# Attention of a fused kernel in plain float32 on quarters of TensorE's array, with scores and values in one stretch

## The chip, the cores and the metric

One core of a Trainium2 chip runs one program. The metric is the device time of one execution in microseconds (us), the median of the runs shown. Engines are named as the profile names them: PE is TensorE (PEld its weight load), DVE VectorE, ACT ScalarE, POOL GpSimd, and SP SyncE, which only issues DMAs here.

## The reference

Banded attention with a bias by distance, then an MLP whose activation is a ratio of two polynomials, on 8 x 576 = 4608 tokens:

```python
scores = q @ k.T / sqrt(64)              # 8 batches, 8 heads, 576 positions, head size 64
mask = (0 <= rel) & (rel < 128)          # rel = query position - key position
p = softmax(where(mask, scores - slope[h] * abs(rel), -1e9))
x = (p @ v)                              # heads side by side: 4608 tokens x 512
h = x @ w_in                             # 512 x 2048, float64 given
P = a0 + a1*h + a2*h*h + a3*h*h*h
Q = 1 + abs(b0)*abs(h) + abs(b1)*h*h
out = (P / (Q + 1e-6)) @ w_out           # 2048 x 512
```

## The kernel before

The 4608 tokens are 36 blocks of 128. The MLP goes over tiles of blocks, `MLP = [3] + [2]*15 + [3]`. Tile 0 is computed with float32 matmuls. From tile 1 on, an operand is a sum of a high and a low part in a rounded type (fp32r), and a product is three matmuls: hi x hi, lo x hi, hi x lo (up, L603; down, L659). The float64 weights arrive as pairs of 32-bit words and are put together on the chip by `convert(k)`, k = 0 to 31 (POOL L560, ACT L561, DVE L562 and L563), whose PSUM tile `cv` lies in the banks `sc0` and `sc1` for k >= 4. This work fills the time of tile 0. `split(k)` then makes the high and low parts.

Attention runs one tile ahead of the MLP: that of tile t+1 is issued among the matmuls of tile t. Its unit is a pair of heads p (heads 2p and 2p+1, whose 64 channels each fill the 128 partitions) and one or two query blocks. A query of block i sees only keys of blocks i-1 and i, so one 128 x 128 matrix holds all of its weights: keys of its own block on and under the diagonal, and keys of the block ahead over it. For each unit:

- `job(u)` loads keys and queries into `kq_raw` (L384) and the values into `v` (L385). From tile 1 on ACT makes `kq_hi` (L386) and DVE `kq_lo` (L387).
- Scores (L430): for each block and head a matmul over 64 rows, one row half of PE's array for each head, against 256 keys, three times (hi x hi, lo x hi, hi x lo), into the banks `sc0` and `sc1`.
- DVE merges the two blocks of keys with a predicated copy (L444) and takes bias and maximum (L450); ACT exponentiates (L455); DVE makes the reciprocal of the sum (L463, L464); POOL multiplies (L465).
- PE transposes the four matrices into `pt` (L476), ACT copies them to `p_all` (L480), and POOL parts them again into own and previous block with two affine selects (L484).
- Values (L509): float32 matmuls over 128 keys, one column half of the array (64 columns) for each head, into `px`. `px` and `pt` take turns in one bank, `ptx`. ACT copies `px` to `x_hi` (L520), DVE makes `x_lo` (L522).

A float32 matmul stands as two records in the trace, an fp32r matmul as one. Scores and values of a unit stand at different places of PE's order, each among matmuls of the MLP on the whole array.

The order of each engine comes from `Plan`, a list scheduler in Python that runs when the program is built: each operation has a due time and an estimated cost, and at each step an engine takes the ready operation that is due first and whose buffers are free. Due times come from constants (`A0` to `BL`, L265 to L271). Each engine then runs its instructions in that order and waits at each for its inputs.

## Time and profile before

| what | us |
|---|---|
| median of 3 runs (lowest, highest) | 1065.49 (1064.55, 1065.85) |
| the profiled execution's span, first to last instruction | 1062.6 |
| PE busy in it | 1037.1 (98%) |
| DVE busy | 834.6 (79%) |
| ACT busy | 707.4 (67%) |
| POOL busy | 520.4 (49%) |
| start, to the first up-projection of tile 0 | 41.2 |
| from there to the last down-projection of tile 0 | 110.2 |
| from there to the last matmul | 907.0 |
| after it | 4.2 |

The span is 2.9 us under the median of the runs. Busy times are sums over the span; the stretches in the lower half of the table differ in what limits them, so each is read by itself. PE's overlapping matmuls count once in its busy time, but a group's mean duration counts the whole way of one matmul through the array, so the pace of a row of matmuls is read from the distance of their starts.

### The profile page before, as it was taken

What the parts mean: (1) busy time and instruction counts of PE and PEld (TensorE: products, weight loads), DVE (VectorE), ACT (ScalarE), POOL (GpSimd) and SP (SyncE); (2) the same over time, 40 slices, a digit from 0 to 9 for tenths busy, and PEclk for the clock granted to TensorE, in tenths of its full rate; (3) what the DMA queues carried; (4) which work ended last, traced back from release to release, by engine and by line L of the source; (5) the groups of instructions that cost most, each with busy time, mean ns of one, the idle gap of its engine ahead of it and who ended that gap; (6) DMA issues with size and microseconds to landing.
All of it is one profiled execution on the core that took longest, in us unless ns stands there. A gap on an engine that the chain in (4) does not pass through costs nothing.

```text
span 1062.6 us, 19670 instructions
## 1 busy us (share of the span) xinstructions
PE 1037.1 (98%) x6863; PEld 861.3 (81%) x6863; DVE 834.6 (79%) x1989; ACT 707.4 (67%) x1642; POOL 520.4 (49%) x578
## 2 busy tenths in 40 slices
PE   7799899999999999999999999999999999999998
PEld 4554467888888888888888888888888888888997
DVE  4798799978787877878787868687878787786776
ACT  5676788666766666757575757666666766685664
POOL 3744579744544453545353444444444545454442
PEclk8899999999999999999999999999999999999999
DMA  9625421011111120202020111112121211020000
GB/s 304 226 70 179 139 92 53 24 58 38 64 40 63 41 75 27 80 24 75 21 72 29 60 52 48 63 33 68 38 73 34 68 43 58 28 74 6 21 1 30
DMA packets 45267, 68.78 MB, mean 65 GB/s; under 512 B 4464, under 2 KB 29936, under 8 KB 45168
## 3 DMA queue, kind: packets, MB, share of 16 engines
q1 hardware_dynamic: 45168, 67.52, 19.8%
q8 instruction: 54, 0.88, 0.3%
q14 instruction: 45, 0.37, 0.1%
HBM read 58.07 MB, written 9.44 MB: 64 GB/s over the span
## 4 chain that ended last, share of the span: by engine, by line
PE 85%; DVE 4%; DMA 4%; POOL 3%; ACT 2%; issue 1%; SPq 0%; DVEq 0%; POOLq 0%; ACTq 0%
PE h L603 36%; PE acc L659 35%; PE px L509 6%; PE sc L430 5%; PE pt L476 2%; DMA raw_w<-in_w_in 2%; POOL w_lo L578 1%; DMA raw_w<-in_w_out 1%; DVE w L563 1%; DMA kq_raw<-in_kqv 1%; POOL p_all L484 1%; POOL g_q L629 0%; ACT pr L455 0%; DVE cv L562 0%; DVE g_p L630 0%
## 5 line engine op out<-in xcount | busy, mean ns | idle before, releaser
L603 PE MATMUL h<-x_hi,wi_hi 128*128 128x256 f32 (+1 forms) x1024 | 308.2, 301 | 0.0
L603 PE MATMUL h<-x_lo,wi_hi 128*128 128x256 f32 (+1 forms) x1024 | 290.7, 284 | 0.0
L627 POOL TENSOR_SCALAR g_q<-g_u,babs 128x512 f32<-128x512 f32 (+1 forms) x152 | 116.0, 763 | 330.1 <-ACT g_u L626 321.0
L603 PE MATMUL h<-x_hi,w_lo 128*128 128x256 f32 (+1 forms) x960 | 272.6, 284 | 0.7 <-POOL w_lo L578 0.7
L603 PEld LDWEIGHTS h<-x_hi,wi_hi 128*128 128x128 f32 x1024 | 192.4, 188 | 39.1 <-issue 8.8
L603 PEld LDWEIGHTS h<-x_lo,wi_hi 128*128 128x128 f32 x1024 | 192.6, 188 | 37.4 <-issue 1.0
L659 PE MATMUL acc<-wo_hi,g_h 128*128 128x512 f32 x528 | 209.0, 396 | 1.3 <-ACT g_h L643 1.3
L659 PE MATMUL acc<-w_lo,g_h 128*128 128x512 f32 x495 | 194.9, 394 | 0.0
L659 PE MATMUL acc<-wo_hi,g_l 128*128 128x512 f32 x528 | 193.3, 397 | 0.0
L629 POOL TENSOR_TENSOR g_q<-g_q,g_u 128x512 f32<-128x512 f32 (+1 forms) x152 | 188.5, 1240 | 9.6
L603 PEld LDWEIGHTS h<-x_hi,w_lo 128*128 128x128 f32 x960 | 181.2, 189 | 1.2 <-POOL w_lo L578 0.9
L626 ACT ACTIVATE g_u<-h 128x512 f32<-128x512 f32 (+1 forms) x152 | 87.4, 575 | 136.0 <-PE h L603 134.6
L635 DVE SCALAR_TENSOR_TENSOR g_q<-g_q,h 128x512 f32<-128x512 f32 (+1 forms) x152 | 99.4, 654 | 81.4 <-ACT h L634 80.1
L632 ACT ACTIVATE g_u<-g_q,guard 128x512 f32<-128x512 f32 (+1 forms) x152 | 107.0, 704 | 69.1 <-POOL g_q L629 68.2
L630 DVE TENSOR_TENSOR g_p<-h,g_p 128x512 f32<-128x512 f32 (+1 forms) x152 | 100.5, 661 | 53.0 <-ACT g_p L628 52.6
L644 DVE TENSOR_TENSOR g_l<-h,g_h 128x512 fp32r<-128x512 f32 (+1 forms) x136 | 90.9, 668 | 51.4 <-ACT g_h L643 49.9
L484 POOL TENSOR_SCALAR_AFFINE_SELECT p_all<-p_all 128x512 f32<-128x512 f32 (+1 forms) x144 | 95.9, 667 | 71.2 <-ACT p_all L480 66.7
L455 ACT ACTIVATE pr<-pr,st 128x128 f32<-128x128 f32 x288 | 112.8, 396 | 13.5 <-DVE st L450 13.4
L465 POOL TENSOR_TENSOR pr<-pr,st 128x512 f32<-128x512 f32 (+1 forms) x76 | 76.6, 1008 | 84.8 <-DVE st L464 55.3
L628 ACT ACTIVATE g_p<-h,na 128x512 f32<-128x512 f32 (+1 forms) x152 | 114.9, 756 | 0.0
L636 DVE SCALAR_TENSOR_TENSOR h<-g_p,na,h 128x512 f32<-128x512 f32 (+1 forms) x152 | 109.3, 719 | 0.0
L631 DVE SCALAR_TENSOR_TENSOR g_p<-g_p,na,h 128x512 f32<-128x512 f32 (+1 forms) x152 | 108.1, 711 | 1.0
(76 smaller groups left out, 1799.9 us busy)
## 6 DMA issues: line engine op xcount, KB each, us to landing
kq_raw<-in_kqv SPq DMA_DIRECT2D x64, 320.0 KB, 2.9
v<-in_kqv SPq DMA_DIRECT2D x68, 192.0 KB, 2.5
out<-o SPq DMA_DIRECT2D x33, 256.0 KB, 2.2
raw_w<-in_w_in SPq DMA_DIRECT2D x16, 512.0 KB, 5.4
raw_w<-in_w_out SPq DMA_DIRECT2D x16, 512.0 KB, 4.0
bias_t<-in_bias SPq DMA_DIRECT2D x44, 64.0 KB, 2.3
kq<-in_kqv SPq DMA_DIRECT2D x4, 320.0 KB, 4.9
kq_raw<-in_kqv SPq DMA_DIRECT2D x4, 192.0 KB, 2.4
```

The costliest lines, as they stand in the source:

```text
L455: nc.scalar.activation(ap(pr)[:, y, :], ap(pr)[:, y, :], AF.Exp, bias=ap(st)[:, y : y + 1], scale=-1.0, accum_out=ap(st)[:, 4 + y : 5 + y])
L484: plan.op(A + D2 + 0.6 - 0.1 * k, cost, lambda e, k=k, sign=sign: nc.gpsimd.affine_select(out=side(k), in_=side(0), pattern=[[0, 2], [0, m ...
L603: nc.tensor.matmul(h(n), w[:, k, :], x[:, k, :], start=(k == 0 and m == 0), stop=(k == NKC - 1 and m == len(seq) - 1))
L627: plan.op(E, {"g": tsc}, lambda e: nc.gpsimd.tensor_scalar(v(g_q), v(g_u), ap(babs)[:, 1:2], ap(babs)[:, 0:1], ALU.mult, ALU.add), reads=[ ...
L628: plan.op(E, {"a": act(W, 1, 2) - 20}, lambda e: nc.scalar.activation(v(g_p), v(h_s), AF.Identity, bias=ap(na)[:, 2:3], scale=ap(na)[:, 3: ...
L629: plan.op(E, {"g": ttc}, lambda e: nc.gpsimd.tensor_tensor(v(g_q), v(g_q), v(g_u), ALU.mult), reads=[(g_q, 0), (g_u, 0)], writes=[(g_q, 0)])
L630: plan.op(E, {"v": dve(W)}, lambda e: nc.vector.tensor_tensor(v(g_p), v(h_s), v(g_p), ALU.mult), reads=[(h_s, 0), (g_p, 0)], writes=[(g_p, ...
L631: plan.op(E, {"v": dve(W, 1)}, lambda e: stt(v(g_p), v(g_p), ap(na)[:, 1:2], v(h_s), ALU.add, ALU.mult), reads=[(h_s, 0), (g_p, 0)], write ...
L632: plan.op(E, {"a": act(W, 0, 1)}, lambda e: nc.scalar.activation(v(g_u), v(g_q), AF.Ln, bias=guard, scale=1.0), reads=[(g_q, 0)], writes=[ ...
L635: plan.op(E, {"v": dve(W)}, lambda e: stt(v(g_q), v(g_q), GUARD, v(h_s), ALU.add, ALU.mult), reads=[(g_q, 0), (h_s, 0)], writes=[(g_q, 0)])
L636: plan.op(E, {"v": dve(W, 1)}, lambda e: stt(v(h_s), v(g_p), ap(na)[:, 0:1], v(h_s), ALU.add, ALU.mult), reads=[(g_p, 0), (h_s, 0)], write ...
L659: nc.tensor.matmul(ap(accs[t][i]), x[:, sl], w, start=(c == 0 and part == 0 and m == 0), stop=(c == NFC - 1 and (part == 1 or t == 0) and ...
```

## The change

All of attention is in plain float32, and `kq_hi` and `kq_lo` are gone. The array is used in quarters of 64 rows x 64 columns. A unit is now always two blocks (two of one pair, or one block of two pairs), which makes 6, 15 x 4 and 6 units, where there were 8, 15 x 4 and 8. For a unit's scores each quarter (row half = head h, column half = half g of the queries) multiplies 192 keys per block: in one piece for g = 0, in pieces of 128 and 64 for g = 1, so that keys which a query half can't see are left out. For its values each quarter (row half = half b of the keys, column half = head) takes four matmuls of 128, 128, 64 and 64 columns. From tile 1 on, the values of unit u-2 and the scores of unit u are one operation of the plan, in the same PSUM tile `sc` of two banks, of which there is one; columns 384 to 511 of each bank hold the values. `pt` is alone in `ptx`.

```diff
+    def values(u, bank):
+        (v, w, w2), keys = stage[u]
+        def run():
+            for n, (own, k, part) in enumerate(((1, 0, 0), (0, 1, 0), (0, 0, 1), (1, 1, 1))):
+                for b in range(2):
+                    r = slice(64 * b, 64 * b + 64)
+                    for h in range(2):
+                        c = slice(64 * h, 64 * h + 64)
+                        q = slice(3 * P + 64 * k, 3 * P + 64 * k + 64) if part else slice(3 * P, 4 * P)
+                        y = ap(w2)[r, k, h] if part else ap(w)[r, 2 * P * k + P * h : 2 * P * k + P * h + P]
+                        nc.tensor.matmul(bank(b)[c, q], ap(v)[r, own, k, c], y, start=(n == 0), stop=(n == 3), tile_position=(64 * b, 64 * h))
+        return run
...
+        back = u - LAG if u - LAG >= first_unit[1] else None
+        if back is not None:
+            small.append(values(back, bank))
...
+            def scores():
+                for b in range(2):
+                    for g, k0, w, at in ((0, 0, 192, 0), (1, 128, 128, 0), (1, 64, 64, 128)):
+                        for h in range(2):
+                            r, c = slice(64 * h, 64 * h + 64), slice(64 * g, 64 * g + 64)
+                            nc.tensor.matmul(bank(h)[c, 192 * b + at : 192 * b + at + w], qt(b)[r, c], kt(b)[r, k0 : k0 + w], start=True, stop=True, tile_position=(64 * h, 64 * g))
...
+        plan.op(A, {"p": cost}, lambda e: [f() for f in small], reads=reads, writes=sk, rows=0.9)
```

The values of a unit of tile 0 stay an operation of their own. The two affine selects become a multiplication by a mask into `p_far` and a subtraction, of 256 elements a partition each. The masks come by one more DMA at the start, cast by DVE; the predicated copies wait for them too. `v` is loaded by four DMAs of 64 partitions instead of one of 128:

```diff
-                plan.op(A + D2 + 0.6 - 0.1 * k, cost, lambda e, k=k, sign=sign: nc.gpsimd.affine_select(out=side(k), in_=side(0), pattern=[[0, 2], [0, m], [sign, P]], compare_op=ALU.is_ge, fill=0.0, base=k - 1, channel_multiplier=-sign), reads=[(w, 0)], writes=[(w, k)])
+        plan.op(A + D2 + 0.5, cost, lambda e: nc.gpsimd.tensor_tensor(ap(w2), mixed(), far(), ALU.mult), reads=[(w, 0), (masks, 0)], writes=[(w2, 0)])
+        plan.op(A + D2 + 0.6, cost, lambda e: nc.gpsimd.tensor_tensor(mixed(), mixed(), ap(w2), ALU.subtract), reads=[(w2, 0), (w, 0)], writes=[(w, 0)])
...
+        plan.op(-7, {"s": 182}, lambda e: eng[e].dma_start(ap(masks16), bias[4, :, :2]), writes=[(masks16, 0)])
+        plan.op(-7, {"v": 300}, lambda e: nc.vector.tensor_copy(ap(masks), ap(masks16)), reads=[(masks16, 0)], writes=[(masks, 0)])
...
+            for g in range(2):
+                eng[e].dma_start(ap(v)[64 * b : 64 * b + 64, :, g], part[64 * g : 64 * g + 64].rearrange("r (j c) -> r j c", j=2))
```

`cv` of the conversions moves into the two banks of `sc`, k even and odd of a chunk in one tile, and the plan's constants are new:

```diff
-        cv = slot(ps1, [P, DM], I32, "cv", tag=f"acc{k % 2}" if k < 4 else f"sc{k % 2}")
+        elif k % 2 == 0:
+            cv_s = cvs[c] = slot(ps1, [P, 2, DM], I32, "cv", tag="sc")
...
-    AOFF, D2, D3, JL, VL = -0.563, 3.406, 5.885, 9.935, 4.671
+    AOFF, D2, D3, JL, VL = -0.5917, 3.483, 6.45, 11.305, 4.987
```

PE in the steady part, before: the values of one unit (L509) and, further on, the scores of another (L430), among up-projections (L603) and down-projections (L659).

```order
L603 MATMUL h<-x_hi,w_lo_1418 128x256
L509 MATMUL px<-p_all,v 64x256 x2
L509 MATMUL px<-p_all,v 64x128 x4
L603 MATMUL h<-x_hi,wi_hi 128x256
...
L603 MATMUL h<-x_hi,w_lo_1457 128x256
L430 MATMUL sc_4864<-kq_hi 128x256
L430 MATMUL sc_4866<-kq_hi 128x256
L430 MATMUL sc_4864<-kq_lo,kq_hi 128x256
L430 MATMUL sc_4866<-kq_lo,kq_hi 128x256
L430 MATMUL sc_4864<-kq_hi,kq_lo 128x256
L430 MATMUL sc_4866<-kq_hi,kq_lo 128x256
```

PE in the steady part, after: one stretch of values (L409) and scores (L463), among up-projections (now L625) and down-projections (L681).

```order
L681 MATMUL acc_4629<-wo_hi,g_l 128x512
L409 MATMUL sc<-p_all,v 64x128 x8
L409 MATMUL sc<-p_far,v 64x64 x8
L463 MATMUL sc<-kq 64x192 x2
L463 MATMUL sc<-kq 64x128 x2
L463 MATMUL sc<-kq 64x64 x2
L463 MATMUL sc<-kq 64x192 x2
L463 MATMUL sc<-kq 64x128 x2
L463 MATMUL sc<-kq 64x64 x2
L625 MATMUL h<-x_hi,wi_hi 128x256
```

The two stretches of a unit have become one, the six matmuls of 128 keys have become sixteen of 64, and the twelve fp32r matmuls of 256 keys twelve float32 matmuls of 64 to 192.

SP at the start of the program, before: keys and queries of four pairs, then values one DMA at a time, `id_sb` (the identity) and the first weights (`raw_w`).

```order
L364 DMA kq_first<-in_kqv 128x256 x3
L310 DMA bias_first<-in_bias 128x1024
L364 DMA kq_first<-in_kqv 128x256
L365 DMA v_first<-in_kqv 128x128
L373 DMA kq_96<-in_kqv 128x640
L365 DMA v_first<-in_kqv 128x128
L308 DMA id_sb<-in_ident 128x256
L365 DMA v_first<-in_kqv 128x128
L373 DMA kq_122<-in_kqv 128x640
L365 DMA v_first<-in_kqv 128x128
L555 DMA raw_w_131<-in_w_in 128x4x256
```

SP at the start, after:

```order
L379 DMA kq<-in_kqv 128x2x384 x2
L384 DMA v<-in_kqv 64x2x128 x4
L377 DMA kq<-in_kqv 128x640
L316 DMA bias_first<-in_bias 128x1024
L384 DMA v<-in_kqv 64x2x128 x4
L312 DMA id_sb<-in_ident 128x256
L313 DMA masks_113<-in_bias 128x256
L384 DMA v<-in_kqv 64x2x128 x4
L377 DMA kq<-in_kqv 128x640
L577 DMA raw_w_139<-in_w_in 128x4x256
```

The masks are the fourteenth DMA. The first weights are the twentieth, where they were the thirteenth.

DVE during tile 0, before: conversions (L562, L563) of `w_9` and `w_8` lie apart, the ratio (L630 to L639) between them.

```order
L562 SCALAR_TENSOR_TENSOR cv<-raw_w,cv 128x512
L639 SCALAR_TENSOR_TENSOR g_839<-g_q,h 128x384
L563 SCALAR_TENSOR_TENSOR w_9_841<-raw_w,cv 128x512
L630 TENSOR_TENSOR g_p<-h,g_p 128x384
L631 SCALAR_TENSOR_TENSOR g_p<-g_p,na,h 128x384
...
L562 SCALAR_TENSOR_TENSOR cv<-raw_w,cv 128x512
L563 SCALAR_TENSOR_TENSOR w_8_797<-raw_w,cv 128x512
```

DVE during tile 0, after:

```order
L584 SCALAR_TENSOR_TENSOR cv<-raw_w,cv 128x512
L585 SCALAR_TENSOR_TENSOR w_8_1001<-raw_w,cv 128x512
L652 TENSOR_TENSOR g_p<-h,g_p 128x384
L584 SCALAR_TENSOR_TENSOR cv<-raw_w,cv 128x512
L653 SCALAR_TENSOR_TENSOR g_p<-g_p,na,h 128x384
L585 SCALAR_TENSOR_TENSOR w_8_1001<-raw_w,cv 128x512
```

Both halves of `w_8` (of w_in and of w_out) are now converted one behind the other, with both banks of `sc` taken for them.

## Rows read from the trace of the kernel before

**Rows 1.** The windows view: for each of four stretches of the span its length, busy time and instructions of each engine, TensorE's granted clock (1.00 is 2.4 GHz), DMA share and GB/s. The stretches are the first three of the table above. The last row is the first 10 us by themselves.
```profile
0.00:41.20 41.20, 30.54 (x172) 18.10 (x172) 24.96 (x105) 24.49 (x84) 20.86 (x33) 0.79 0.89 297
41.20:151.40 110.20, 103.34 (x410) 55.86 (x408) 93.52 (x216) 77.70 (x175) 59.20 (x74) 0.98 0.39 122
151.40:1058.40 907.00, 903.16 (x6286) 787.33 (x6284) 715.44 (x1668) 604.86 (x1385) 440.31 (x474) 1.00 0.15 47
...
0.00:10.00 10.00, 7.02 (x29) 3.28 (x30) 1.93 (x15) 3.30 (x10) 1.43 (x6) 1.00 0.70 202
```

**Rows 2.** The waits of PE, from 41.2 to 151.4 (two rows) and the largest from 151.4 to 1058.4 (one row): operation and what it waited for, us in total, how often, the longest.
```profile
PE h L603 <- DVE g L639: 4.9, 5, 1.7
PE px L509 <- POOL p_all L484: 1.9, 1, 1.9
...
PE acc L659 <- ACT g_h L643: 1.3, 2, 0.8
```

**Rows 3.** The timeline of PE around the scores of one unit: start, us, engine, line, operation, records. Matmuls of the MLP on the whole array stand at both ends.
```profile
301.91 0.28 PE L603 MATMUL h<-x_hi,w_lo 128*128 128x256 f32 x1
302.12 0.39 PE L430 MATMUL sc<-kq_hi 64*128 64x256 f32 x2
302.34 0.28 PE L430 MATMUL sc<-kq_lo,kq_hi 64*128 64x256 f32 x2
302.46 0.28 PE L430 MATMUL sc<-kq_hi,kq_lo 64*128 64x256 f32 x2
...
303.02 0.39 PE L603 MATMUL h<-x_hi,wi_hi 128*128 128x256 f32 x1
303.24 0.28 PE L603 MATMUL h<-x_lo,wi_hi 128*128 128x256 f32 x1
```

**Rows 4.** The same view around the values of one unit.
```profile
315.77 0.28 PE L603 MATMUL h<-x_hi,w_lo 128*128 128x256 f32 x1
315.98 1.09 PE L509 MATMUL px<-p_all,v 128*64 128x256 f32 x12
...
317.22 0.28 PE L603 MATMUL h<-x_lo,wi_hi 128*128 128x256 f32 x1
```

**Rows 5.** PE's instructions from 41.2 to 1058.4 by line and shape: names, tile, records, busy us, mean ns of one, idle before. Of the scores, the hi x hi records stand for the other two products, which have as many.
```profile
L509 PE MATMUL px<-p_all,v 128*64 128x128 f32 x530 | 41.6, 276 | 0.0
L430 PE MATMUL sc<-kq_hi 64*128 64x256 f32 x236 | 40.3, 334 | 0.0
L476 PE MATMUL pt<-id_sb,pr 128*128 128x128 f32 x264 | 40.0, 273 | 1.0 <-POOL pr L465 1.0
L509 PE MATMUL px<-p_all,v 128*64 128x256 f32 x240 | 39.3, 406 | 2.8 <-POOL p_all L484 2.7
...
L430 PE MATMUL sc<-kq_hi 64*128 64x128 f32 x24 | 3.5, 288 | 0.0
```

**Rows 6.** The chain that ended last, at two places of tile 0: start, us, what, records. The first row is eight records of float32 matmuls of 512 columns, the second four transposes.
```profile
66.91 3.43 PE acc L659 x8
...
72.49 0.44 PE pt L476 x4
```

**Rows 7.** The values of another unit, twelve records of 128 columns in two column halves: the timeline of PE over all of it, then what of L509 is in flight at 505.31, and what weight loads are at 505.15.
```profile
504.98 0.88 PE L509 MATMUL px<-p_all,v 128*64 128x128 f32 x12
505.78 0.73 PE L659 MATMUL acc<-wo_hi,g_l 128*128 128x512 f32 x2
...
505.13 0.39 PE L509 MATMUL px<-p_all,v 128*64 128x128 f32 x4
...
505.03 0.25 PEld L509 LDWEIGHTS px<-p_all,v 128*64 128x64 f32 x4
```

**Rows 8.** The start: PE's first up-projection in its timeline, and SP's issue of `id_sb`.
```profile
41.19 1.99 PE L609 MATMUL h<-x_hi,w 128*128 128x256 f32 x8
...
4.55 0.43 SPq L308 DMA_DIRECT2D id_sb<-in_ident  x1
```

**Rows 9.** Instructions of DVE and POOL from 151.4 to 1058.4, and of ACT and DVE from 0 to 41.2, by line and shape, columns as in Rows 5.
```profile
L450 DVE CUSTOM_DVE_ANT_0 pr<-sc,bias_std 128x128 f32<-128x128 f32 x162 | 39.2, 283 | 0.0
L444 DVE COPY_PREDICATED sc<-id_sb,sc 128x256 f32<-128x256 uint32 x90 | 35.6, 420 | 2.4 <-PE sc L430 2.4
L522 DVE TENSOR_TENSOR x_lo<-px,x_hi 128x256 fp32r<-128x256 f32 x59 | 24.5, 415 | 1.5 <-ACT x_hi L520 1.0
L450 DVE DVE_READ_ACCUMULATOR2_ANT st<- 128x1 f32 x236 | 19.2, 81 | 0.0
...
L629 POOL TENSOR_TENSOR g_q<-g_q,g_u 128x512 f32<-128x512 f32 x120 | 156.2, 1301 | 7.0
...
L484 POOL TENSOR_SCALAR_AFFINE_SELECT p_all<-p_all 128x512 f32<-128x512 f32 x118 | 79.9, 677 | 63.6 <-ACT p_all L480 59.8
L465 POOL TENSOR_TENSOR pr<-pr,st 128x512 f32<-128x512 f32 x58 | 61.3, 1057 | 69.9 <-DVE st L464 42.7 <-ACT h L634 21.9 <-PE h L603 5.1
...
L455 ACT ACTIVATE pr<-pr,st 128x128 f32<-128x128 f32 x28 | 10.9, 394 | 5.1 <-DVE st L450 5.0
L455 ACT ACTIVATION_READ_ACCUMULATOR pr<-pr,st 128x1 f32 x28 | 5.3, 190 | 0.0
L480 ACT COPY p_all<-pt 128x512 f32<-128x512 f32 x4 | 2.3, 585 | 1.3 <-PE pt L476 1.3
...
L562 DVE SCALAR_TENSOR_TENSOR cv<-raw_w,cv 128x512 int32<-128x512 int32 x7 | 4.6, 684 | 0.3 <-ACT cv L561 0.3
```

More of the change, by code (lines that the diff above doesn't have):

```diff
@@ L48, in bias_tables @@
 def bias_tables():
-    out = np.empty((4, P, H, P), np.float32)
+    out = np.zeros((5, P, H, P), np.float32)
     slopes = 2.0 ** (-8.0 * (np.arange(H, dtype=np.float32) + 1) / H)
@@ new lines, in out_values @@
+    def out_values(u, A, src, sk):
+        t, items = units[u]
+        if t not in xs:
+            xs[t] = [slot(const, [P, NKC, P * MLP[t]], F32 if t == 0 else F32R, "x_hi", tag=f"x_hi{t % 2}"),
+                     slot(const, [P, NKC, P * MLP[t]], F32R, "x_lo", tag=f"x_lo{t % 2}") if t else None]
+        xh, xl = xs[t]
+        (p0, n0), (p1, n1) = items
+        c0 = (n0 - MSTART[t]) * P
+        if p0 == p1:
+            into = lambda x: ap(x)[:, p0, c0 : c0 + 2 * P].rearrange("q (b c) -> q b c", b=2)
+        else:
+            into = lambda x: ap(x)[:, p0 : p0 + 2, c0 : c0 + P]
+        if t == 0:
+            for b, (p, n) in enumerate(items):
+                plan.op(A + 0.3, {"a": act(P, 1)}, lambda e, b=b: nc.scalar.copy(into(xh)[:, b], src(b)), reads=[sk[b]], writes=[(xh, items[b])])
+            return
+        plan.op(A + 0.3, {"a": act(2 * P, 1)}, lambda e: nc.scalar.copy(into(xh), src()), writes=sk + [(xh, k) for k in items])
+        plan.op(A + 0.4, {"v": dve(2 * P)}, lambda e: nc.vector.tensor_sub(into(xl), src(), into(xh).bitcast(F32)),
+                reads=sk + [(xh, k) for k in items], writes=[(xl, k) for k in items], follows=[raws[k] for k in range(16, 2 * NFC, 2)] if t == 2 else ())
@@ L397, in attention @@
     def attention(u):
-        t, p, j = units[u]
-        m = TILES[j]
-        kinds = [block_type(STARTS[j] + i) for i in range(m)]
-        kt, qt, vt, parts, kq_keys, v_keys = job(u)
         A = a_time(u)
+        if u < first_unit[1] and u % 2:
+            banks = [slot(ps1, [P, 4 * P], F32, f"sc{h}", tag=f"acc{h}") for h in range(2)]
+            bank = lambda h: ap(banks[h])
+            sk = [(banks[0], 0), (banks[1], 0)]
+        else:
+            sc = slot(ps1, [P, 2, 4 * P], F32, "sc")
+            bank = lambda h: ap(sc)[:, h]
+            sk = [(sc, 0), (sc, 1)]
@@ L485, in attention @@
-        if t not in xs:
-            xs[t] = [slot(const, [P, NKC, P * MLP[t]], F32 if t == 0 else F32R, "x_hi", tag=f"x_hi{t % 2}"), slot(const, [P, NKC, P * MLP[t]], F32R, "x_lo", tag=f"x_lo{t % 2}") if t else None]
-        px = slot(ps3, [P, 2, P], F32, "px", tag="h") if t == 0 else slot(ps1, [P, 2, P], F32, "px", tag="ptx")
-        xh, xl = xs[t]
-        runs = []
-        for b in range(m + 1):
-            ends = [i for i, half in ((b - 1, 1), (b, 0)) if 0 <= i < m and (half or kinds[i] != 1)]
-            if ends:
-                runs.append((b, ends[0], ends[-1] + 1))
@@ L497, in attention @@
-        runs.sort(key=lambda r: r[1] - r[2])
-        full = runs[0][2] - runs[0][1] == m
-        if not full:
-            runs.sort()
-        def values(e):
-            for n, (b, i0, i1) in enumerate(runs):
-                new = n == 0 if full else n == 0 or i0 >= runs[n - 1][2]
-                done = n == len(runs) - 1 or not full and runs[n + 1][1] >= i1
-                c0 = 2 * b - 1 if i0 == b - 1 else 2 * b
-                for h in range(2):
-                    r = slice(64 * h, 64 * h + 64)
-                    nc.tensor.matmul(ap(px)[r, i0:i1], vt(b)[:, r], ap(w)[:, h, c0 : c0 + i1 - i0], start=new, stop=done, tile_position=(0, 64 * h))
@@ L521, in attention @@
-        if t:
-            plan.op(A + D3 + 0.4, {"v": dve(m * P)}, lambda e: nc.vector.tensor_sub(into(xl), src(), into(xh).bitcast(F32)),
-                    reads=[(px, 0), (xh, (p, j))], writes=[(xl, (p, j))], follows=[raws[k] for k in range(16, 2 * NFC, 2)] if t == 2 else ())
-    def x_keys(t, ks, js=None):
-        return [(x, (k, j)) for x in xs[t] if x for k in ks for j in range(len(TILES)) if MSTART[t] <= STARTS[j] < MSTART[t] + MLP[t] and (js is None or j in js)]
+                for k in range(2):
+                    nc.tensor.transpose(ap(pt)[:, k, h], ap(pr)[:, k, 2 * h : 2 * h + 2].rearrange("q b c -> q (b c)"), ap(id_sb)[:, 0])
```

251 lines of the change are left out of this document (121 added, 130 removed).

## The prediction, made before the changed kernel ran

> **What bounds the kernel now.** I read the windows view by stretch first [rows 1]. In the 907.0 us behind tile 0 PE is busy for 903.16 at the full granted clock, and DVE, ACT and POOL for 715, 605 and 440. So PE's instructions set the time there, and 3.8 us are idle, the largest wait 1.3 [rows 2]. During tile 0 (110.2 us) PE is busy for 103.3; of the 6.9 us of idle time the waits for DVE's ratio make 4.9 and one for POOL 1.9 [rows 2]. The first 41.2 us are another thing: PE is busy for 30.5 at a mean clock of 0.79 and no engine is full. So the change is worth what it takes out of PE's row of instructions from 41.2 on, plus what it does to the first 41.2 us. What the other engines do counts only where it makes PE wait.
>
> **PE from 41.2 on, what goes.** Work of the MLP follows at fixed distances, so a stretch of attention costs the distance by which it pushes the next MLP matmul back. Scores: from the MLP matmul at 301.91 to the second one behind the stretch, at 303.24, are 1.33 us, of which two MLP matmuls take 2 x 0.1175 (the steps between 302.34 and 302.46 and their like): 1.10 is the stretch, made of six steps of 0.1175 (0.705) and 0.39 at its edges [rows 3]. Values, by the same reading: 317.22 - 315.77 - 0.235 = 1.21 [rows 4]. The pace of float32 comes from eight records of 512 columns in 3.43 us, 0.84 ns a column and record [rows 6]; a normal unit's 1024 record-columns in each column half take 0.86, and 0.35 are edges: the array drains (0.09), loads the first weights (0.05), and does the same on the way back (0.20). Counts [rows 5]: scores 3 x 236 records of 256 keys and 3 x 24 of 128, two at a time, are (354 x 0.1175) + (36 x 0.107) = 45.5; by the code they stand in 67 stretches (one was done before 41.2), so edges are 67 x 0.39 = 26.1; sum 71.6. Values: 240 x 256 and 528 x 128 record-columns over two halves at 0.84 ns are 54.2, and 68 x 0.35 are 23.8; sum 78.0. Together **149.6 us** go.
>
> **PE from 41.2 on, what comes.** 66 units of tiles 1 to 16, two with their scores ahead of the up-projection, so 66 stretches hold 64 scores and 66 values. Each quarter of the array gets 2 x 192 columns of scores and 128 + 128 + 64 + 64 of values, 384 each, two records: 768 x 0.84 = 0.645 us if the four quarters run at once. That is not in the trace of before; column halves are. Twelve records of 128 columns go through in 0.80 us [rows 7], where one at a time would need 12 x 0.1075 = 1.29; after a first step of 0.16 the next pair follows at 0.109, so two run at once at full pace, and four records are in flight at 505.31 [rows 7]. Bounds for a normal stretch are 1.29 (all four quarters at once) and 2.58 (two at a time). I take 1.29, since the moving operand of four quarters is the same 256 rows an instant as that of two column halves. Edges: 0.35, as for values today, and 0.05 for one more exposed first load at the turn from values to scores (0.16 - 0.109). So 66 x 0.40 + 130 x 0.645 = 26.4 + 83.9 = **110.3 us**. A full stretch is 1.69, against 1.10 + 1.21 = 2.31 before. Transposes fall from 264 [rows 5] to 260; four take 0.44 [rows 6], so 0.4 goes. Net on PE: 110.3 - 149.6 - 0.4 = **-39.7 us**.
>
> A row speaks for the weight loads staying hidden: at 505.15 four loads of column halves, begun at 505.03, run while matmuls over the same 128 rows are in flight, and the steps stay at 0.109 [rows 7]. The Trainium skill, "TensorE: Matmul & The Clock Gate", section "Part 3: Packing small matmuls — row/col tiling", says that a load overlaps with matmuls in flight only when its row group differs. Two quarters share each row half, so by that rule loads would be exposed here; rows 7 contradict it for column halves. The sum by the row is the one above, by the rule that of the second rival.
>
> **The cover of that.** A stretch now needs the one tile `sc`: DVE must have finished two predicated copies, four maxima and `x_lo` of the stretch ahead. By today's rows that is 2 x 0.42 + 4 x (0.283 + 0.081) + 0.415 = 2.7 us [rows 9]. In the new order the MLP matmuls between two stretches, at today's durations, give at least 7.4 us in the steady part, so 4.7 us of cover are left; if a stretch came sooner PE would stand still by the difference. Values wait two units, 15 us or more, for exponentials, transposes and POOL. POOL's two affine selects (2 x 0.677 [rows 9]) become two operations on 256 elements; the 512-element product at 1.30 is the nearest row, and half of it, 0.65, makes them equal. DVE loses `kq_lo` and ACT `kq_hi`. SP gets 480 DMAs where it had 271; at its distance of 0.475 us that is 228 us of 1062, and loads are asked for 11 us or more ahead. All this is nothing on the path. The idle 3.8 us behind tile 0 I leave.
>
> **Tile 0.** By the new order about 11 of these 39.7 us lie in tile 0. The conversions on DVE, two of 0.68 for each k [rows 9], must be done before the last down-projections, and they now take both banks of `sc`, for two k at once, behind the attention. So a part of those 11 us can turn into waits. Bounds: all idle time of tile 0 gone (-7), or 5 us more. I take 0.
>
> **The start.** The masks are the fourteenth DMA, behind about 2.03 MB; at the 202 GB/s of the first 10 us [rows 1] they land at about 10.0, where `id_sb`, issued at 4.55 [rows 8], did for this work before. Then six units of 2 x 0.42 + 4 x 0.364 = 2.3 on DVE (13.8) and one conversion (1.4) bring 25.2. Behind the last maximum come four exponentials of 0.394 + 0.190, POOL's product 1.06, transposes 0.44, the copy 0.585 [rows 9], two POOL operations of 0.65, values and the copy to `x_hi` (1.4): 7.1, so 32.3 with nothing in the way. Today it is 41.2 [rows 8], with 25.0 us of DVE work in it [rows 1]. Bounds 33 and 45 (eight more DMAs ahead of the first weights at 0.475 each, 3.8 us late); I take the middle of 33 and 41.2, **37**: -4.2.
>
> **The sum.** 1062.6 - 39.7 - 4.2 = 1018.7 us of span. The span is 2.9 under the median, so 1021.6: **1022 us**, 4.1% faster.
>
> **Rivals.**
> 1. Unequal pieces keep the quarters in step. If a matmul can't end ahead of the one issued before it, 192 columns of g = 0 cover the 128 of g = 1, and the 64 stand alone: 256 steps in place of 192 for each block. That is 64 x 2 blocks x 2 records x 0.84 = 0.215 a stretch, 64 x 0.215 = 13.8: **1036**. For it: pairs in rows 3 and 7 always have equal lengths, so the trace shows no unequal ones. Against it: the pieces go to quarters and banks of their own, and column halves each keep their full pace. The page named above says in the same section that matmuls end strictly in the order of issue, which would bring this about; no row of before tells.
> 2. The slower end: each pass of a quarter shows its weight load. A quarter loads up to 16 times in a stretch (8 for values, 8 for the scores of g = 1), at the 0.05 of an exposed load: 0.80, so 66 x 0.80 = 53: **1075**, slower than before. It decides from a stretch of 1.69 + 43.7/66 = 2.35 us on. Against it is rows 7, where only the first step shows it; but a quarter's load has half as many columns beside it to hide under.
> 3. Only two quarters run at once: 130 x 0.645 = 84 more, **1106**.
> 4. Tile 0 and the start give the gain back: up-projection at 45 (+8) and 5 us of waits for conversions: **1035**. Speaking for it: nearly all of DMA's time is taken in the first 41 us [rows 1].
> 5. The change would do nothing if attention on PE were hidden; rows 1 exclude that behind tile 0.
>
> **How the numbers follow.** Forecast 0.67 (1022, own range 1008 to 1030), rival 1 0.13, rival 4 0.10, rival 2 0.06, rival 3 0.04. The low end takes in an early start (33) and tile 0 without idle time: 1022 - 4 - 7 = 1011, and 3 for the turn from values to scores costing nothing: 1008. The high end takes in rivals 1 and 4 together (1049); the slower ones stay out. Range 1008 to 1050. A measurement of this kernel can tell about 0.2% from no change. Faster by more 0.89 (forecast, 1, 4 and a part of 2), slower 0.09, within 0.02.
>
> **What would show it.** In the changed profile: a full stretch pushes the MLP matmuls by 1.7 us (1.9: rival 1; 2.5: rival 2; 3.0: rival 3); PE's busy time behind tile 0 is down by some 35 us and its idle time there stays under 5; the first up-projection starts at 33 to 41. The forecast is wrong if PE waits for `sc` or for POOL's `p_far` in the steady part, or if idle time in tile 0 grows by more than 10 us.

## The result, and the profile after

The changed kernel takes 1039.82 us (median of 4 runs, 1038.86 to 1040.95) where the kernel before takes 1065.34 beside it (4 runs): a ratio of 0.9764, with a 95% interval of 0.975 to 0.9778. It is 25.5 us faster. The forecast was 43.5 us faster (1022), with a range of 1008 to 1050: direction and range held, the size was off by 18 us. In the profiled executions the span falls from 1062.6 to 1039.1, by 23.5 where the prediction has 43.9 (39.7 on PE and 4.2 at the start), so 20.4 us have to be found. (The profiled execution of the changed kernel is the longest of its four, 1.1 us above their median.) "The first up-projection" is, here and in the tables ahead, that of blocks 1 and 2; block 0's alone comes at 20.30 before and at 28.12 now.

The timeline of PE of the changed kernel around one stretch of attention (start, us, engine, line, operation, records) answers to [rows 3, 4]. `sc<-p_all,v` and `sc<-p_far,v` are the values of one unit, `sc<-kq` (counted with its smaller pieces) the scores of another:

```profile
403.06 0.40 PE L681 MATMUL acc<-wo_hi,g_l 128*128 128x512 f32 x1
403.39 0.67 PE L409 MATMUL sc<-p_all,v 64*64 64x128 f32 x16
403.88 0.41 PE L409 MATMUL sc<-p_far,v 64*64 64x64 f32 x16
404.11 0.85 PE L463 MATMUL sc<-kq 64*64 64x192 f32 x24
404.89 0.39 PE L625 MATMUL h<-x_hi,wi_hi 128*128 128x256 f32 x1
405.11 0.28 PE L625 MATMUL h<-x_lo,wi_hi 128*128 128x256 f32 x1
...
405.35 0.40 PE L681 MATMUL acc<-wo_hi,g_h 128*128 128x512 f32 x1
405.58 0.40 PE L681 MATMUL acc<-w_lo,g_h 128*128 128x512 f32 x1
```

A down-projection's step is 0.23 (405.35 to 405.58), an up-projection's 0.1175. So the stretch is 405.11 - 403.06 - 0.233 - 0.1175 = 1.70 us; the median of the 58 whole stretches is 1.698. The prediction has 1.69. Less the 0.40 of edges that the prediction has, 1.30 are left for 1536 record-columns in each quarter, 0.85 ns a column, close to the 0.84 of [rows 6]: all four quarters run at once.

The same trace with the matmuls of L409 in flight between 403.60 and 403.62, its weight loads between 403.55 and 403.70, and the scores (L463) in flight between 404.30 and 404.35 (operation and count; ns, minimum, median and maximum; first and last start; shapes):

```profile
L409 PE MATMUL sc<-p_all,v x8: 269/294/320, 403.4 to 403.6; 64*64 64x128 f32 x8
...
L409 PEld LDWEIGHTS sc<-p_all,v x12: 132/133/133, 403.4 to 403.7; 64*64 64x64 f32 x12
...
L463 PE MATMUL sc<-kq x9: 216/272/325, 404.1 to 404.3; 64*64 64x192 f32 x4, 64*64 64x128 f32 x4, 64*64 64x64 f32 x1
```

Eight records are in flight while twelve loads pass beside them. Of the scores, a piece of 64 columns has already begun while pieces of 192 are still in flight, so the quarters aren't kept in step.

The windows view, one row each for the first 10 us, the start up to the first up-projection, tile 0 up to 148.9, and the rest up to the last matmul (columns as in rows 1, to which they answer); then a part of that rest by itself; and in PE's timeline the first up-projection, which answers to [rows 8], and the last down-projection of tile 0:

```profile
0.00:10.00 10.00, 5.95 (x63) 3.28 (x63) 0.12 (x3) 1.28 (x1) 0.20 (x4) 1.00 0.66 204
0.00:44.70 44.70, 29.77 (x436) 23.23 (x437) 25.23 (x112) 23.17 (x85) 22.10 (x33) 0.73 0.87 270
44.70:148.90 104.20, 91.50 (x473) 48.99 (x471) 86.39 (x185) 71.64 (x156) 57.83 (x71) 1.00 0.46 142
148.90:1034.90 886.00, 880.15 (x8319) 783.81 (x8317) 683.04 (x1620) 581.68 (x1333) 444.36 (x468) 1.00 0.17 52
...
148.90:162.40 13.50, 9.44 (x89) 6.33 (x87) 12.20 (x26) 8.44 (x22) 13.50 (x12) 0.87 0.22 65
...
44.68 1.99 PE L631 MATMUL h<-x_hi,w 128*128 128x256 f32 x8
...
161.55 1.02 PE L681 MATMUL acc<-w,g 128*128 128x512 f32 x2
```

Three things differ from [rows 1] against the forecast. The first up-projection starts at 44.68 instead of 41.19, where 37 was predicted. PE's idle time in tile 0 up to 148.9 is 104.20 - 91.50 = 12.7, where it was 6.9. And PE's busy time from the first up-projection to the last matmul falls by only (103.34 + 903.16) - (91.50 + 880.15) = 34.9 instead of 39.7, with 5.85 idle behind 148.9 (3.84 before).

148.9 isn't the end of tile 0's work, though: three of its 48 down-projections stand later in the changed order, the last at 161.55, and 13.50 - 9.44 = 4.1 of the 5.85 lie ahead of its end. Up to the last down-projection, as [rows 1] has tile 0, idle time is 16.8 (6.9 before), and behind it 1.8 (3.84 before). The sum, 18.6 against 10.7, is the same.

The waits of the changed kernel (operation and what it waited for; us, times, longest), first of PE over the whole span, then of its weight loads from 160 to 1030:

```profile
PE h L625 <- DVE g L661: 7.6, 7, 1.8
...
PE h L625 <- DVE w L585: 3.1, 1, 3.1
...
PEld sc L409 <- issue: 9.7, 31, 0.4
PEld acc L681 <- ACT o L709: 5.3, 13, 0.4
```

The wait for DVE's `w` (a conversion) is new against [rows 2], and the one for the ratio `g` is longer (6.4 of the 7.6 lie between 44.7 and 148.9; in tile 0 it was 4.9). `acc <- ACT o` comes 13 times, once for each tile behind the first few; the trace of before has none of them. It stands with the weight loads, and PE counts as busy meanwhile. One such place, in the timelines of PE, ACT and DVE:

```profile
275.51 0.40 PE L681 MATMUL acc<-wo_hi,g_l 128*128 128x512 f32 x1
275.99 0.50 PE L681 MATMUL acc<-wo_hi,g_h 128*128 128x512 f32 x1
276.33 0.39 PE L681 MATMUL acc<-w_spare,g_h 128*128 128x512 f32 x1
...
275.35 0.59 ACT L709 COPY o<-acc 128x512 f32<-128x512 f32 x1 [0.18 <-PE acc L681]
...
275.22 0.68 DVE L666 TENSOR_TENSOR g_l<-h,g_h 128x512 fp32r<-128x512 f32 x1
```

The steps from 275.51 are 0.48 and 0.34 instead of 0.23 each: 0.36 lost. PE's first down-projection of the next tile needs the bank that ACT copies until 275.94. And DVE's `g_l`, which ends at 275.90, reads the bank that the next up-projection writes. Two waits end within 0.04 us of each other.

So the 20.4 us are: start 44.7 - 37 = 7.7; idle time up to 148.9 12.7 - 6.9 = 5.8; idle time behind that 5.85 - 3.84 = 2.0; and 4.9 that PE's busy time hides, of which 13 x 0.36 = 4.7 are these boundaries. Less those 4.7, PE's busy time is 34.9 + 4.7 = 39.6 shorter, where -39.7 was forecast.

### The profile page after: what moved, and what is told of

Read it like the earlier page. It is cut to its first block, busy times and chain, and to the rows that moved or that the text cites. A ratio compares the mean times of both kernels' runs of the same rounds, so it can differ in the third digit from the quotient of the medians.

```text
span 1039.1 us, 24386 instructions
## 1 busy us (share of the span) xinstructions
PE 1001.4 (96%) x9223; PEld 856.0 (82%) x9223; DVE 795.0 (77%) x1916; ACT 677.0 (65%) x1572; POOL 524.3 (50%) x570
## 3 DMA queue, kind: packets, MB, share of 16 engines
HBM read 63.11 MB, written 9.44 MB: 70 GB/s over the span
## 4 chain that ended last, share of the span: by engine, by line
PE 86%; DVE 4%; DMA 3%; ACT 2%; SPq 2%; POOL 2%; issue 1%; DVEq 0%; POOLq 0%; ACTq 0%
PE h L625 38%; PE acc L681 37%; PE sc L409 5%; PE sc L463 4%; PE pt L524 3%; DMA raw_w<-in_w_out 2%; SPq L384 1%; ACT o L709 1%; DVE w_lo L600 1%; DMA kq<-in_kqv 1%; DVE h L658 0%; POOL g_q L651 0%; DVE g_q L657 0%; DMA raw_w<-in_w_in 0%; DVE cv L584 0%
## 5 line engine op out<-in xcount | busy, mean ns | idle before, releaser
L625 PE MATMUL h<-x_hi,wi_hi 128*128 128x256 f32 (+1 forms) x1024 | 304.3, 297 | 1.9 <-DVE g L661 1.2
L625 PE MATMUL h<-x_lo,wi_hi 128*128 128x256 f32 (+1 forms) x1024 | 292.3, 285 | 0.0
L625 PE MATMUL h<-x_hi,w_lo 128*128 128x256 f32 (+1 forms) x960 | 273.4, 285 | 0.0
L625 PEld LDWEIGHTS h<-x_lo,wi_hi 128*128 128x128 f32 x1024 | 193.2, 189 | 34.7 <-issue 1.9
L625 PEld LDWEIGHTS h<-x_hi,wi_hi 128*128 128x128 f32 x1024 | 193.5, 189 | 28.2 <-issue 3.1
L681 PE MATMUL acc<-wo_hi,g_h 128*128 128x512 f32 x528 | 209.4, 397 | 1.1
L681 PE MATMUL acc<-wo_hi,g_l 128*128 128x512 f32 x528 | 196.7, 398 | 0.0
L681 PE MATMUL acc<-w_lo,g_h 128*128 128x512 f32 x495 | 195.0, 394 | 0.0
L625 PEld LDWEIGHTS h<-x_hi,w_lo 128*128 128x128 f32 x960 | 181.5, 189 | 0.0
L514 POOL TENSOR_TENSOR pr<-pr,st 128x512 f32<-128x512 f32 x72 | 76.4, 1060 | 157.3 <-DVE st L513 90.8
L658 DVE SCALAR_TENSOR_TENSOR h<-g_p,na,h 128x512 f32<-128x512 f32 (+1 forms) x152 | 109.6, 721 | 0.0
L681 PEld LDWEIGHTS acc<-wo_hi,g_h 128*128 128x128 f32 x528 | 99.2, 188 | 9.1 <-ACT o L709 5.3
```

The costliest lines, as they stand in the source:

```text
L625: nc.tensor.matmul(h(n), w[:, k, :], x[:, k, :], start=(k == 0 and m == 0), stop=(k == NKC - 1 and m == len(seq) - 1))
L658: plan.op(E, {"v": dve(W, 1)}, lambda e: stt(v(h_s), v(g_p), ap(na)[:, 0:1], v(h_s), ALU.add, ALU.mult), reads=[(g_p, 0), (h_s, 0)], write ...
L681: nc.tensor.matmul(ap(accs[t][i]), x[:, sl], w, start=(c == 0 and part == 0 and m == 0), stop=(c == NFC - 1 and (part == 1 or t == 0) and ...
```

## The experiments

Each kernel is the changed one with one edit (or an earlier one of these with one more, as said), made on the finished order where it moves something, so that all the rest stays as planned. Times are medians of runs beside the kernel before; the changed kernel's 1039.8 (ratio 0.9764) is the mark.

**What holds the start.** SP issues one DMA after the other. Its timeline in the kernel before (first row, the first weights) and in the changed kernel (`SPq`; a row of x4 is four issues):

```profile
6.44 0.43 SPq L555 DMA_DIRECT2D raw_w<-in_w_in  x1
...
1.73 2.65 SPq L384 DMA_DIRECT2D v<-in_kqv  x4
...
5.54 2.55 SPq L384 DMA_DIRECT2D v<-in_kqv  x4
8.13 0.59 SPq L312 DMA_DIRECT2D id_sb<-in_ident  x1
8.77 0.43 SPq L313 DMA_DIRECT2D masks<-in_bias  x1
...
12.47 0.43 SPq L577 DMA_DIRECT2D raw_w<-in_w_in  x1
...
16.66 1.88 SPq L315 DMA_DIRECT2D bias_std<-in_bias  x1
```

A values DMA takes 0.65 (four from 5.54 to 8.13), not 0.475. The masks, without which DVE can't begin, are issued at 8.77 and the first weights at 12.47, 6.0 us later than before. Theory A has it that the row of values DMAs as a whole holds the start; theory B, that the masks alone do; and the start may be bound elsewhere.

*masks_first*: the loads of the masks and of `id_sb` ahead of the first values.

```diff
     order = plan.order()
+    at = min(order.index(o) for o in v_loads)
+    order = order[:at] + first_loads + [o for o in order[at:] if o not in first_loads]
```

> The changed kernel with one move: SP issues id_sb and the masks ahead of the first v load instead of behind two of them; every other engine's order is the same. Theory A (SP's queue as a whole makes the start late: sixteen v loads at 0.65 us each stand ahead of the bias tables and most weights): the masks land near 4.5 instead of 11, but bias_first, the first weights and bias_std are issued as late as before, so the first up-projection of blocks 1 and 2 comes at 43 to 45 (44.7 in the changed kernel) and the time is 1038 to 1040 us. Rival B (DVE's wait of 10.09 us for the masks is what makes the start late): up-projection at about 39.5, time about 1035.

1039.8 us (0.9764, 0.975 to 0.9777). DVE begins 5 us sooner and then waits again, in DVE's timeline:

```profile
5.93 0.30 DVE L316 CAST masks<-masks 128x256 f32<-128x256 bf16 x1 [5.00 <-DMA masks<-in_bias]
...
10.74 0.29 DVE L502 CUSTOM_DVE_ANT_0 pr<-sc,bias_first 128x128 f32<-128x128 f32 x1 [3.51 <-DMA bias_first<-in_bias]
```

The up-projection comes at 45.44. The masks alone aren't it: `bias_first` now lands about as late (10.74) as they did (11.02).

*v_one_dma*: the values lie in memory as in the tile, so that the four DMAs of a unit become one (two where a unit is two pairs).

```diff
-            part = src[:, 0, N + b * P : N + (b + 2) * P] if two else src[:, b, N:]
-            for g in range(2):
-                eng[e].dma_start(ap(v)[64 * b : 64 * b + 64, :, g], ...
+            row = ap(v).rearrange("q j g c -> q (j g c)")
+            if not two:
+                eng[e].dma_start(row[64 * b : 64 * b + 64], v_src[b])
+            elif b == 0:
+                eng[e].dma_start(row, v_src)
```

> The changed kernel with the values laid out in memory as the tile has them, so that a unit of one pair loads v with one DMA of 128 x 2 KB instead of four of 64 x 2 x 512 B (units of two pairs: two DMAs); orders of all engines are the same but for these DMAs. Theory A (SP's queue makes the start late): bias_std is issued at about 9 instead of 16.7, the first up-projection of blocks 1 and 2 comes at about 38 instead of 44.7, time about 1033 us. Rival B (only the masks count): they are issued 3.4 us sooner, up-projection at 41, time about 1036. Rival C (the start is bound by DMA bandwidth or by DVE, not by SP): within 1 us of 1040.

1036.93 us (0.9734, 0.9721 to 0.9747). `bias_std` is issued at 10.01 instead of 16.66, and the up-projection starts at 41.16, 3.5 us sooner; the time from there to the last matmul, 989.2, is that of the changed kernel (989.8). So SP's issues held the start by some 3.5 us (2.9 in the medians), not by all of the 7.7, and the whole gain that theory A asks for didn't come. The up-projection is back where the kernel before has it (41.19). These are also the numbers that rival B gives; against B speak *masks_first* and the next run, where DVE begins earlier still. PE's timeline, and the windows view of this kernel from 10 to 30 us, which shows what comes up behind the issues:

```profile
41.16 1.99 PE L636 MATMUL h<-x_hi,w 128*128 128x256 f32 x8
...
10.00:20.00 10.00, 6.98 (x88) 6.13 (x92) 7.37 (x47) 5.51 (x24) 5.09 (x7) 0.53 1.07 379
20.00:30.00 10.00, 7.52 (x98) 5.74 (x94) 8.04 (x24) 8.54 (x31) 8.74 (x12) 0.67 1.03 388
```

The DMA engines are now full (1.07 and 1.03; 0.75 in the changed kernel from 10 to 20 us), as they are in the kernel before (1.03 and 0.95).

*loads_sorted*: *v_one_dma* with the first loads in the order in which they are needed, and the values of tile 0's first four units behind the first weights. F says that the order of the loads holds the rest, G that their bytes do.

```diff
+    moved = first_loads[::-1] + std_load + early
...
+    order = head + first_loads[::-1] + rest[: third + 1] + std_load + rest[third + 1 : raw + 1] + early + rest[raw + 1 :]
```

> v_one_dma with SP's first loads in the order in which their results are needed: keys and queries of two units, bias_first, masks, id_sb, keys and queries, bias_std, keys and queries, first weights, and only then the values of tile 0's first four units (six DMAs). Other engines' orders are unchanged. Theory F (the start goes by when the first tables land, since DVE stood idle until 9.9 us in v_one_dma): DVE begins at about 5.5, the first up-projection of blocks 1 and 2 comes at 36 to 38 instead of 41.2, time about 1033 us. Theory G (from 10 us on the DMA engines are full, so the start goes by all the bytes ahead of the up-projection, in whatever order): 40 to 42 and 1036 to 1038.

1036.37 us (0.9733, 0.972 to 0.9747), the up-projection at 40.44 in PE's timeline:

```profile
40.44 1.99 PE L638 MATMUL h<-x_hi,w 128*128 128x256 f32 x8
```

DVE begins at 6.86 (9.89 in *v_one_dma*), and of these three us at most 0.7 arrive, which the medians (0.6 apart, with all but the same interval) don't tell from nothing. Nearer to G: the DMA engines are full at 1.03, 1.04 and 0.98 in the three windows from 10 to 40 us.

A rival that needs no run of its own is TensorE's clock. In the changed kernel the granted clock is 0.55 from 10 to 20 us and 0.50 (the level of 1.2 GHz) from 20 to 30, having fallen while PE stood waiting for DVE; before, it is 0.50 and 0.99. But four kernels below do the same work up to the up-projection (*down_later*, *g_l_first*, *both_at_boundary* and *split_stretch*) and start it at 43.50, 44.44, 44.94 and 45.46, with mean clocks up to there of 0.80, 0.81, 0.73 and 0.81. The start doesn't follow the clock. Their spread, 2 us, is also how far one profile can be trusted on the start: the 0.8 us by which *masks_first* is late and the 0.7 here lie within it, while *v_one_dma* with 41.16 lies 2.3 below all four.

**Whether the one stretch carries the gain.** *split_stretch*: the scores stand behind the next MLP operation, as in the kernel before; quarters, pieces and tiles stay.

```diff
-        plan.op(A, {"p": cost}, lambda e: [f() for f in small], ...
+        o = plan.op(A, {"p": cost}, lambda e: small[0](), ...
+        if len(small) == 2:
+            seconds.append((o, small[1]))
...
+            if id(o) in later:
+                later[id(o)]()
```

> The changed kernel with the scores of a stretch behind the next operation of the MLP in PE's order (three up-projections or two down-projections), so that values and scores of quarters stand apart; nothing else moves. Theory A (a stretch pays 0.35 us at its edges, so that putting values and scores together is worth 0.30 to 0.35 us each time): 64 x 0.32 = 20 us more, 1060 us. Rival E (the gain comes from the quarters alone, edges are cheap between quarters and the whole array): under 5 us more, 1040 to 1045.

1064.17 us (0.9989, 0.998 to 0.9998), 24.3 us above the changed kernel. A unit in its timeline of PE:

```profile
411.31 0.40 PE L685 MATMUL acc<-wo_hi,g_l 128*128 128x512 f32 x1
411.64 0.67 PE L409 MATMUL sc<-p_all,v 64*64 64x128 f32 x16
412.13 0.41 PE L409 MATMUL sc<-p_far,v 64*64 64x64 f32 x16
412.47 0.38 PE L629 MATMUL h<-x_hi,wi_hi 128*128 128x256 f32 x1
412.69 0.28 PE L629 MATMUL h<-x_lo,wi_hi 128*128 128x256 f32 x1
412.81 0.28 PE L629 MATMUL h<-x_hi,w_lo 128*128 128x256 f32 x1
413.01 0.90 PE L465 MATMUL sc<-kq 64*64 64x192 f32 x24
413.84 0.50 PE L685 MATMUL acc<-wo_hi,g_h 128*128 128x512 f32 x1
414.18 0.40 PE L685 MATMUL acc<-w_lo,g_h 128*128 128x512 f32 x1
```

Values cost 412.69 - 411.31 - 0.35 = 1.03, scores 414.18 - 412.81 - 0.35 = 1.02: 2.05 in place of 1.70. The pair of edges that the second stretch adds is 0.35, and 64 of them are 22.4 of the 24.3 us. So the quarters without the one stretch leave the kernel 0.1% from where it was. That doesn't make them worthless: a unit costs PE 2.31 us before, 2.05 here and 1.70 in one stretch, so the quarters save 0.26 and the stretch 0.35. The 17 us of the quarters (64 x 0.26) are what this kernel, much like the changed one, loses elsewhere: 4.3 at its start (45.46 instead of 41.19), some 7 in idle time and some 6 at the tile boundaries.

**The tile boundaries.** The view of waits names ACT's copy of `acc`. The rival is that it isn't what holds PE, or that another wait stands right beside it.

*down_later*: the first down-projection of each tile stands behind the next up-projections, when the copy is done.

```diff
+    for o in firsts:
+        at = order.index(o)
+        to = next(n for n in range(at + 1, len(order)) if order[n].engine == "p")
+        order[at : to + 1] = order[at + 1 : to + 1] + [o]
```

> The changed kernel with PE's first down-projection of each tile from tile 2 on behind the next group of up-projections (0.35 us) instead of ahead of it; nothing else moves. Theory A (PE stands still 0.41 us in each of 13 tiles for ACT's copy of the finished accumulator, since the new tile's first down-projection takes the same bank): the wait goes, time 1040 - 13 x 0.41 = 1034.5 us. Rival D (the 0.41 us are not a wait of the path, or come back at the next matmul): 1039 to 1041.

1040.06 us (0.9765, 0.9751 to 0.9778): nothing. In its timelines of PE and DVE the stop is there still, now at the up-projection (273.79 to 274.32, 0.53), and it ends as `g_l` does, at 274.17:

```profile
273.79 0.40 PE L681 MATMUL acc<-wo_hi,g_l 128*128 128x512 f32 x1
274.32 0.36 PE L625 MATMUL h<-x_hi,wi_hi 128*128 128x256 f32 x1
...
273.49 0.68 DVE L666 TENSOR_TENSOR g_l<-h,g_h 128x512 fp32r<-128x512 f32 x1
```

The view of waits names `PE acc` for it; what ends just before PE goes on is `g_l`. So the copy alone isn't it. H: both waits must go, and either alone gives nothing.

*both_at_boundary*: *down_later*, and DVE makes `g_l` ahead of the operation of L658 (another pair's product) at those 13 places. *g_l_first*: the exchange on DVE alone (M: it gives the gain by itself).

```diff
+        low = max(n for n in range(to) if order[n] in lows)
+        top = max(n for n in range(low) if order[n].engine == "v")
+        if order[top] in tops:
+            order.insert(top, order.pop(low))
```

> down_later with one more exchange on DVE at each of these places: the low part g_l of the ratio (which is the last to read the h bank that the next up-projection takes) stands ahead of another pair's product instead of behind it, 0.68 us sooner. Theory H (two waits end within 0.04 us of each other at a tile's boundary, ACT's copy of the accumulator and DVE's g_l, so that taking away one alone gave nothing): PE's 0.3 to 0.4 us of standing still at 13 boundaries go, time about 1035 us. Rival I (the ratio's chain is late as a whole, and the next link makes PE wait as long): 1039 to 1041.

> The changed kernel with only the exchange on DVE of both_at_boundary (g_l ahead of another pair's product at 13 boundaries), the first down-projection where it was. Theory H (two waits end within 0.04 us of each other, so either edit alone gives nothing): 1039 to 1041 us, PE still stands for ACT's copy at each boundary. Rival M (g_l alone was the wait): about 1036.

*both_at_boundary* takes 1036.61 us (0.9738, 0.9724 to 0.9751), *g_l_first* 1039.91 (0.9762, 0.9747 to 0.9778). H is right, M fell. From the first up-projection to the last matmul are 985.5 us with both edits, 989.4 and 988.9 with one of them, 989.8 with none: the boundaries cost some 4 us (3.2 in the medians). The weight loads' waits of *both_at_boundary* have no row `acc <- ACT o` any more, and in PE's timeline there the steps are 0.24:

```profile
PEld sc L409 <- issue: 11.2, 42, 0.4
PEld sc L409 <- PE pt L524: 3.2, 13, 0.2
...
274.84 0.40 PE L681 MATMUL acc<-wo_hi,g_l 128*128 128x512 f32 x1
275.08 0.28 PE L625 MATMUL h<-x_hi,wi_hi 128*128 128x256 f32 x1
```

**Tile 0.** *conversions_cut* leaves three of the four operations of half of the conversions out (POOL's, ACT's and DVE's first), so that half of the weights are other numbers. J: the conversions stand in the way of the ratio, and its waits go with them; K: the ratio's own chain is too long for PE, and little changes.

```diff
-        plan.op(T, {"g": 840}, lambda e: eng[e].tensor_scalar(top()...
-        plan.op(T, {"a": 700}, lambda e: nc.scalar.activation(cv(), ...
-        plan.op(T + 1, {"v": 603}, lambda e: nc.vector.scalar_tensor_tensor(cv(), top(), 3, ...
+        plan.op(T, {"g": 840}, lambda e: k >= 16 or eng[e].tensor_scalar(top()...
+        plan.op(T, {"a": 700}, lambda e: k >= 16 or nc.scalar.activation(cv(), ...
+        plan.op(T + 1, {"v": 603}, lambda e: k >= 16 or nc.vector.scalar_tensor_tensor(cv(), top(), 3, ...
```

> The changed kernel with the conversions of the weights k = 16 to 31 cut down to one DVE operation each: POOL's and ACT's operation and DVE's first one are left out (48 operations of about 0.7 us each, all in tile 0), so half of the weights are other numbers. Loads and the order of all that is left are unchanged. Theory J (tile 0 is held up because the conversions stand among the links of the ratio's chain on DVE, ACT and POOL; PE's waits for DVE there are 9.5 us): most of these waits go, last down-projection of tile 0 some 8 us earlier, time about 1032 us. Rival K (the ratio's chain with three banks is too long by itself now that PE has less attention in tile 0, or the loads of the weights hold it up): less than 3 us, 1037 to 1040.

1035.47 us (0.9729, 0.9715 to 0.9742), 4.3 below the changed kernel. In the profiles it is 5.4 us shorter from the up-projection to the last matmul. The wait for DVE's `w` falls from 3.1 to 0.2 and that for `g` from 7.6 to 4.7 (PE's waits, whole span):

```profile
PE h L625 <- DVE g L661: 4.7, 8, 1.2
```

That lies between J (1032) and K (1037 to 1040): what is cut of the conversions costs some 5 us, and the 4.7 that are left are about what the kernel before waits for `g` (4.9). The run takes work away; it doesn't put the conversions back where they were. So it doesn't tell whether they come late by their new places (two at once, with both banks of `sc`) or because PE has less attention to do meanwhile.

**Both repairs, and an earlier start.** *combined* is *loads_sorted* with *both_at_boundary*. *conversions_behind* is *combined* with the conversions that stood ahead of the first up-projection, all but those of k = 0 and 2, moved behind it on ACT, DVE and POOL (L: the conversions hold the start, and the up-projection comes at 35 to 37).

```diff
+        if k not in (0, 2):
+            later_convs.extend(conv_ops)
...
+    at = order.index(up_blocks[-1])
+    held = [o for o in order[:at] if o in later_convs]
+    order = [o for o in order[: at + 1] if o not in held] + held + order[at + 1 :]
```

> loads_sorted and both_at_boundary together. Theory H with theory A (start and boundaries are apart and their gains add): 1036.4 - 3.2 = 1033 us. Rival N (the tile 0 that starts sooner waits longer for the weights, or the sorted loads move the boundaries): 1035 or more.

> combined, with the conversions that stand ahead of the first up-projection of blocks 1 and 2 moved directly behind it on ACT, DVE and POOL, all but those of k = 0 and 2; loads and PE's order unchanged. Theory L (the last units of tile 0's attention stand behind these conversions, and the conversions behind their weights' DMAs, so that the start goes by the weights' arrival): the up-projection at 35 to 37 instead of 40.4; 2 to 3 us may come back as waits for the weights of the next chunks; time 1029 to 1032 us. Rival O (attention's own chain of units 4 and 5 sets the start): up-projection at 39 or later, time 1032 to 1035.

*combined*: 1033.16 us (0.9692, 0.9677 to 0.9707), the fastest kernel here: 0.9692 / 0.9764 is 0.7% under the changed one, and the intervals don't meet. Both repairs add up. *conversions_behind*: 1037.33 (0.9743, 0.9725 to 0.9762). Its up-projection starts at 35.89, 4.9 us sooner than in *combined* (40.75), as L says, and all of it is lost: the next transposes wait for POOL, which now does conversions, as its timeline of PE and its view of waits show:

```profile
47.73 1.12 PE L531 MATMUL pt<-id_sb,pr 128*128 128x128 f32 x4 [6.90 <-POOL pr L521]
...
PE pt L531 <- POOL pr L521: 9.9, 4, 6.9
```

From the up-projection to the last matmul it needs 994.6, *combined* 986.2. The sooner up-projection isn't a sooner tile 0. Nor does the run set the conversions apart from the DMAs' bytes: with the conversions, later loads move too (DMA's share is 0.49 from 30 to 35 us and 0.00 from 35 to 40).

## Why the prediction was right in direction and 18 us off

The time lies in the stated range, 1008 to 1050, but not in the forecast's own, 1008 to 1030. The high end came from rivals 1 and 4 together, and rival 1 didn't happen, so that the wide range held is in part luck.

**Right: PE's work.** The stretch (1.69 forecast, 1.70 measured), four quarters at once, the edges, and the counts gave -39.7; -39.6 came. (It counts 528 records where [rows 5] has 530, which is 0.1 us.) *split_stretch* shows the edges by putting them back. Rival 1 (1.9), rival 2 (2.5) and rival 3 (3.0) are excluded by 1.698: the pieces don't keep the quarters in step, and no loads are exposed. In [rows 7] loads of column halves ran beside matmuls over the same rows; twelve loads in 0.15 us beside eight records in flight show it for quarters. The Trainium skill, "TensorE: Matmul & The Clock Gate", section "Part 3: Packing small matmuls — row/col tiling", has it that a load overlaps only where its row group differs, by which a stretch would be 2.5; the measurement decides against that here.

**Right: the cover in the steady part.** Behind 148.9 PE waits for neither `sc` nor POOL by more than one wait of 1.5 us and one of 1.3, both ahead of 162.4.

**Wrong: "All this is nothing on the path".** SP's DMAs were counted at 0.475 and judged over the whole span. In the first 17 us they are one queue ahead of everything, and the values DMAs take 0.65. The bound of 45 has the first weights 3.8 us late, by eight more DMAs (there are seven, the twentieth for the thirteenth); they are issued 6.0 us later. *v_one_dma* shows 3.5 us of the start for SP's issues.

**Wrong: "I take the middle of 33 and 41.2".** The sum for the start followed DVE and the first unit, and took the masks as the only late load. *masks_first* shows that `bias_first` comes next. With the loads in order the start is still 40.4, with DMA full from 10 to 40 us, and *conversions_behind* shows that conversions stand ahead of the up-projection too, and can't be put off for nothing. Of the 7.7 us some 3.5 are shown for SP's issues. The other 4 are the gain on the kernel before that the sum promised, and with the issues repaired it still doesn't come; what keeps it away lies between the DMAs' bytes and the conversions. The upper bound of the text, 45, which is the start of before plus SP's delay, is what came.

**Wrong: "I take 0" for tile 0.** The idle time grew by 5.8 up to 148.9, and by 9.9 up to the last down-projection of tile 0; the bound was 5, and more than 10 was to count against the forecast. *conversions_cut* gives 5.4 back: the conversions, which the prediction named and priced at nothing, are the larger part of it. Whether by their place or by the work that PE no longer does is not shown.

**Wrong: "The idle 3.8 us behind tile 0 I leave."** Idle time behind tile 0 is no longer than it was; what came up are waits that PE's busy time hides, at the tile boundaries: 13 times 0.36, and no part of the sum looked there. *both_at_boundary* gives some 4 back. Why they came up is open: that PE has 0.6 us less work for each unit suggests itself, but *split_stretch*, which gives 0.35 of it back, has them too (`acc <- ACT o`, 6.1 us, 13 times).

The late start and tile 0's waits together are rival 4, which was worked out at 1035 and given 0.10. It is the nearest to what happened; with the boundaries' 4.7 us on top, which it doesn't have, it gives 1040.

**Open.** How the other 4 us of the start divide between bytes and conversions; a kernel that takes fewer bytes in the first 40 us and is the same otherwise was not tried. What the waits for the ratio that *conversions_cut* leaves (4.7) hang on, and where the boundaries' waits come from, was not tried either.
